# Hash attention with a squared-ReLU layer: the next chunk's x asked for one product later, and the last chunk's output stores on one queue

## The chip, the cores and the metric

The kernel runs on one core of one Trainium2 chip. The metric is the device time in microseconds (us) of one execution, here the median of three runs. The profiler's record of one further execution gives the span of that execution and the time of every instruction and transfer in it.

## What is computed

The first part is attention in which a query sees only the keys of its own hash bucket; its output, laid out as 3072 tokens by 512 features, is the input x of a two-layer network. All is in float32.

```
mask   = q_bucket[..., :, None] == k_bucket[..., None, :]
scores = where(mask, scale * q @ k.T, -1e9)          # 4 batches, 8 heads, 768 tokens, 64 features
attn   = softmax(scores) @ v
x      = attn.transpose(0, 2, 1, 3).reshape(3072, 512)
h      = x @ w_in                                    # 512 -> 2048
g      = max(h, 0) ** 2
out    = g @ w_out                                   # 2048 -> 512
```

## The kernel before

**Stages.** The first 330 us compute the attention, pair of heads by pair of heads, and write x to a buffer in device memory (x_all). Beside that the weights are brought in and written back in rearranged form (w_in_7, w_out_1). The rest of the time is the network. It runs over x in three chunks of 1024 tokens (`NCHUNK` = 3, index i). A chunk has a hidden stage, which makes g, and an output stage (`project`), which makes out.

**Fewer multiplications.** Both layers use a scheme of the Strassen and Winograd kind: a matrix product is split in 2 by 2 blocks and done with seven block products in place of eight, at the price of sums and differences of blocks on VectorE before and after. The output layer does this twice over. So an output stage is seven *output products*, k = 0 to 6, and each is itself seven groups of matmuls (function `product`, matmul at L712) that read seven weight tiles called leaf. In the order of TensorE's work the groups of one output product use the operands "11", "21", "t2", "t1", "t3", "22" and "t4". The last group, "t4", reads the block y21 of the product's operand after VectorE has subtracted t2 from it in place; this subtraction is the first line of `hook` (`minus(y21, y21, t2)`, executed at L516). Then `hook` makes the differences that the next product needs (`inner_sums`, L516), and the results of the groups are added up on VectorE (L1008), some copied out by ScalarE (L719).

**Order.** The instructions stand in the order in which the program writes them down (`tc.manual_schedule()`); each engine, and each engine's DMA queue, takes its own in that order. VectorE therefore does nothing that stands behind a waiting instruction, and the same holds for GpSimd (POOL), whose queue issues DMAs one after the other.

**What stands on POOL's queue in the first chunk's output stage.** For k = 0 to 3 `factor_units(k)` prepares a quarter of the inner weights of the later chunks: two loads of 256 KB into tiles named h (L837), then two stores of parts of them (L846), then `sums_a` on VectorE, which reads the loaded tiles (L510 to L513), then two stores of these sums (L846). On VectorE `sums_a` of product k stands ahead of that product's `hook`. In between stands `load_x(i + 1)` (L554), one DMA of 2 MB that brings the next chunk's x into the only x tile; before the change it is written down after product k = 0, so POOL's queue holds: the loads, stores and sums of k = 0, then x, then those of k = 1, of k = 2 and of k = 3. The next chunk's x is first read by `sum_x`, written down after product k = 3.

**Tiles h.** The tag h has five buffers (`NH`), which serve in turn the hidden stage, `factor_units` (four for each k) and the output tiles.

**Output.** When two halves of an output tile are done, `put_out` transposes it on VectorE (L1022) and stores it with four DMAs of 64 KB (L1029), most on SyncE's queue (SP), those of the lower right quarter, (ih, jh) = (1, 1), on POOL's; and in the last chunk the second and fourth DMA of the tile (1, 0) that is stored by `put_out` also on POOL's. The very last tile is stored by `put_last` in halves (L1049): two DMAs on SP's queue and two on ScalarE's (ACT). The leaf tiles are loaded by ACT's queue (L998), x's weights (w_unit) by SP's.

Of the kernel before, what the change touches and what calls it, by code (L numbers as in the profile page):

```python
# [34 lines left out]
def kernel(  # L35
# [10 lines left out]
    nc = tc.nc  # L46
# [20 lines left out]
    NCHUNK = B * S // NCH  # L67
# [447 lines left out]
    def minus(out, in0, in1):  # L515
        nc.vector.tensor_tensor(out=out, in0=in0, in1=in1, op=ALU.subtract)  # L516
# [34 lines left out]
    def load_x(i):  # L551

        x = p_c.tile([P, NFT, NCH], FP32, name="x")
        nc.gpsimd.dma_start(out=x, in_=x_all[:, :, i * NCH:(i + 1) * NCH])  # L554
        xs[i] = x, [p_c.tile([P, 2, NCH // 2], FP32, name=f"t_x{n}") for n in range(3)]
# [36 lines left out]
    with tc.manual_schedule():  # L592
# [21 lines left out]
        for pr in range(NP):  # L614
            a, b = 2 * pr, 2 * pr + 1
# [87 lines left out]
        def product(n, w, at, bt, c11, c12, c21, c22, hook=None):  # L703

            acc = [ps_m.tile([P, 512], FP32, name=f"acc{i}")[:, 0:w] for i in range(3)]

            def add(to, a, b, first, last):  # L710
                for i in range(n):
                    nc.tensor.matmul(  # L712
                        out=acc[to], lhsT=a(i), rhs=b(i), start=first and i == 0,
                        stop=last and i == n - 1, skip_group_check=True,
                    )

            def keep(of, name):
                t = p_r.tile([P, 512], FP32, name=name)[:, 0:w]
                nc.scalar.copy(out=t, in_=acc[of])  # L719
                return t  # L720

            add(0, at(0), bt["11"], True, False)
            one = keep(0, "one")
            add(1, at(1), bt["21"], True, True)
            if hook:
                hook()
            c11(acc[1], one)
            add(0, at(4), bt["t2"], False, False)
            two = keep(0, "two")
            add(2, at(3), bt["t1"], True, False)  # L730
            five = keep(2, "five")
            add(0, at(5), bt["t3"], False, False)
            three = keep(0, "three")
            add(2, at(6), bt["22"], False, True)
            c12(acc[2], two)
            c22(three, five)
            add(0, at(2), bt["t4"], False, True)
            c21(acc[0])
# [94 lines left out]
        def factor_units(n):  # L833

            src = [new_h().rearrange("p (a f c) -> p a f c", a=2, c=P) for _ in range(2)]
            for j in range(2):
                nc.gpsimd.dma_start(out=src[j], in_=w_in_7[j * NQ + n, :, 5:7])  # L837
            sums = [new_h().rearrange("p (a f c) -> p a f c", a=2, c=P) for _ in range(2)]
            sums_a(
                src[0][:, :, 0], src[0][:, :, 1], src[1][:, :, 0], src[1][:, :, 1],  # L840
                *(sums[j // 2][:, :, j % 2] for j in range(4)),
            )
            for lo, hi, t in (
                (0, 2, src[0]), (2, 3, src[1][:, :, 1:2]), (3, 5, sums[0]), (5, 7, sums[1])
            ):
                nc.gpsimd.dma_start(out=w_in_49[n, :, :, lo:hi], in_=t)  # L846

        def load_inner(i, n):

            if n < NQ:  # L850
                w_inner[i, n] = []
                for j, name in enumerate((("sum0", "sum3"), ("sum2", "sum1"))[n % 2]):
                    t = p_y.tile([P, 4, QN], FP32, name=name).rearrange("p a (b c) -> p (a b) c", c=P)
                    nc.sync.dma_start(out=t[:, 0:7], in_=w_in_49[n, :, j])
                    w_inner[i, n].append(t)
# [6 lines left out]
        def sums_inner(i):  # L862

            t_inner[i] = [p_y.tile([P, NQ, QN], FP32, name=f"t{m}", bufs=2) for m in range(2)]
            for j, t in enumerate(t_inner[i]):
                y11, y12, y21, y22 = quarters_x(i, j)
                minus(t[:, 0], y12, y11)
                minus(t[:, 1], y22, t[:, 0])
                minus(t[:, 2], y21, t[:, 1])
                minus(y12, y22, y12)  # L870
# [107 lines left out]
        def inner_sums(k, n=slice(0, NQ)):  # L978

            if k not in tens:  # L980
                tens[k] = [p_y.tile([P, NQ, QN], FP32, name=f"t{m}", bufs=2) for m in range(2)]
            t1, t2 = (t[:, n] for t in tens[k])
            b = OUTER[k][1]
            at = slice(NQ + n.start, NQ + n.stop)
            y11, y12, y21, y22 = b[:, n, 0:QN], b[:, n, QN:HN], b[:, at, 0:QN], b[:, at, QN:HN]
            minus(t1, y12, y11)
            minus(t2, y22, t1)
            minus(y12, y22, y12)
# [3 lines left out]
        def load_leaf(n, early=False):  # L992
            if n < 49:
                k, m = divmod(n, 7)
                m = LEAVES[m]
                leaves[k, m] = p_y.tile([P, NQ, P], FP32, name="leaf", bufs=NLEAF)
                queue = nc.sync if early else nc.scalar
                queue.dma_start(out=leaves[k, m], in_=w_out_49[OUTER[k][0], :, m])  # L998
# [19 lines left out]
        def put_out(i, ih, jh, n, o):  # L1018


            ot = p_r.tile([P, HN], FP32, name="h", bufs=NH)
            nc.vector.transpose(out=ot, in_=o)  # L1022
            m0 = ih * HD + n * P
            at = slice(i * NCH + jh * HN, i * NCH + (jh + 1) * HN)
            for a in range(P // 32):
                queue = nc.gpsimd if (ih, jh) == (1, 1) else nc.sync
                if (i, ih, jh) == (NCHUNK - 1, 1, 0) and a % 2:
                    queue = nc.gpsimd
                queue.dma_start(  # L1029
                    out=out[at, m0 + a * 32:m0 + (a + 1) * 32].rearrange("(c i) j -> i c j", i=32),  # L1030
                    in_=ot[a * 32:(a + 1) * 32].rearrange("i (c j) -> i c j", j=32),
                )
# [21 lines left out]
        def project(i):  # L1054
# [60 lines left out]
            for k in range(7):  # L1115
                b = OUTER[k][1]
                t1, t2 = tens.pop(k)
                if i == 0 and k < NQ:
                    factor_units(k)
                if k == 6 and more:  # L1120
                    load_inner(i + 1, 0)
                at = lambda m, k=k: lambda n: leaves[k, m][:, n]
                bt = {
                    "11": lambda n: b[:, n, 0:QN], "21": lambda n: b[:, NQ + n, 0:QN],
                    "22": lambda n: b[:, NQ + n, QN:HN], "t1": lambda n: t1[:, n],
                    "t2": lambda n: t2[:, n], "t3": lambda n: b[:, n, QN:HN],
                    "t4": lambda n: b[:, NQ + n, 0:QN],
                }

                def hook():  # L1130
                    y21 = b[:, NQ:NR, 0:QN]
                    minus(y21, y21, t2)
                    if k + 1 < 7 and k not in (1, 3):
                        inner_sums(k + 1)
                    if k == 6 and more:
                        sums_inner(i + 1)

                counted = []

                def a_with_load(m, k=k):  # L1140
                    load_leaf(7 * k + len(counted) + NLEAF - 2)
                    counted.append(m)
                    return at(m)

                use = uses[k]
                product(
                    NQ, QN, a_with_load, bt, lambda *p: use(0, *p), lambda *p: use(1, *p),
                    lambda p: use(2, p, None), lambda *p: use(3, *p), hook,
                )
                if k == 0 and i + 1 < NCHUNK:  # L1150
                    load_x(i + 1)
                if k in (3, 4) and i + 1 < NCHUNK:
                    sum_x(i + 1, 2 * k - 5)
                    sum_x(i + 1, 2 * k - 4)
                if k == 5 and i + 1 == NCHUNK:
                    guard()
                if k == 0:

                    for h in range(2):
                        at_h = slice(h * NQ, (h + 1) * NQ)  # L1160
                        minus(b11[:, at_h], b22[:, at_h], b_t[:, at_h])
                    inner_sums(2)
                if k == 2:

                    for h in range(2):
                        at_h = slice(h * NQ, (h + 1) * NQ)
                        minus(b_t[:, at_h], b21[:, at_h], b11[:, at_h])
                    inner_sums(4)
# [43 lines left out]
        for i in range(NCHUNK):  # L1212
# [32 lines left out]
            if i == NCHUNK - 1:  # L1245
                tops()
            project(i)
    fast.close()

# [234 lines left out]
```

## Time and profile before

| what | value |
|---|---|
| time, median of 3 runs | 881.38 us |
| lowest and highest of the 3 | 880.67 and 882.03 us |
| the profiled execution: time, span | 882.09 us, 880.3 us |
| x load (L554), three of them: issue to landing, shortest, median, longest | 9.1, 11.0, 12.6 us |
| loads of `factor_units` (L837), eight of them | 3.3, 5.6, 13.4 us |
| one `put_out` DMA (L1029): issue time on SP, shortest, median, longest | 315, 496, 877 ns |
| the same on POOL | 649, 649, 676 ns |
| last stores (L1049): issue to landing | 4.2 to 4.5 us |

In a line of the timeline the first number is the start in us from the span's start, the second the time until the end of the last of the merged instructions; then come engine, source line, operation, what is written from what is read, and the count. In brackets stands how long the engine had been idle before it and what ended that. A DMA's line on a queue is its issue alone; when it lands is told apart. The source lines are those of the kernel before.

### The profile page before, as it was taken

Reading aid. Unit: us, or ns where it says so; the run is one execution under the profiler, and the core shown is the slowest. Engines: PE = TensorE matmul, PEld = TensorE weight load, DVE = VectorE, ACT = ScalarE, POOL = GpSimd, SP = SyncE. Lnnn points to the kernel's source line nnn. Section 1 sums busy time; section 2 is a strip of 40 time slices with the busy share of each in tenths; the row PEclk is TensorE's granted clock in tenths of the full one; section 3 lists DMA queues with packets and bytes.
Section 4 is the critical chain, followed back from the end, with each engine's and each line's share of the span. In section 5 each row is a group of like instructions: output and inputs, shape, how many; then the busy total and the mean of one; then the engine's idle time right before and its main releaser. Section 6 shows DMA issues by size and latency. Waiting matters only on the chain.

```text
span 880.3 us, 12132 instructions
## 1 busy us (share of the span) xinstructions
PE 865.7 (98%) x4340; PEld 520.4 (59%) x4340; DVE 760.7 (86%) x1099; ACT 391.7 (44%) x673; POOL 106.9 (12%) x172
## 2 busy tenths in 40 slices
PE   8999999999999999999999999999999999999996
PEld 4444444444444444444678865556888755568885
DVE  5899999999999998888779968888889788888875
ACT  5988888888888851222211123332111233321110
POOL 2000000000000000554231021111000211110002
PEclk9999999999999999999999999999999999999999
DMA  9677977898878546999897665436846744355565
GB/s 187 122 151 134 231 151 152 180 259 220 179 169 217 162 130 207 297 262 289 289 342 255 175 160 173 164 114 229 288 145 187 171 159 156 128 167 152 159 172 107
DMA packets 224131, 167.09 MB, mean 190 GB/s; under 512 B 164448, under 2 KB 181344, under 8 KB 224064
## 3 DMA queue, kind: packets, MB, share of 16 engines
q1 hardware_dynamic: 189152, 87.19, 41.6%
q0 software_dynamic: 12528, 41.30, 15.0%
q10 hardware_dynamic: 22384, 37.76, 13.9%
q8 instruction: 36, 0.59, 0.3%
q14 instruction: 31, 0.25, 0.1%
HBM read 124.52 MB, written 41.68 MB: 189 GB/s over the span
## 4 chain that ended last, share of the span: by engine, by line
PE 95%; DVE 2%; ACT 1%; issue 1%; DVEq 0%
PE acc L712 40%; PE st L396 17%; PE acc L931 16%; PE xo L438 13%; PE acc L884 5%; PE hash L346 1%; PE tot L455 1%; DVE total L428 1%; ACT e L413 1%; ACT bits L356 1%; PE xo L326 0%; PE tp L309 0%; DVE s_in L516 0%; DVE out_piece L179 0%; DVE power L171 0%
## 5 line engine op out<-in xcount | busy, mean ns | idle before, releaser
L413 ACT ACTIVATE e<-st 128x1024 f32<-128x1024 f32 x192 | 145.1, 810 | 45.1 <-PE st L396 41.1
L396 PE MATMUL st<-feat,feat 64*128 64x512 f32 (+1 forms) x768 | 150.4, 484 | 0.0
L438 PE MATMUL xo<-e,v_nat 128*64 128x512 f32 (+1 forms) x768 | 134.8, 492 | 0.0
L712 PE MATMUL acc<-b,leaf 128*128 128x256 f32 x600 | 133.3, 380 | 1.5 <-issue 1.5
L712 PEld LDWEIGHTS acc<-b,leaf 128*128 128x128 f32 x600 | 113.9, 190 | 17.9 <-issue 2.7
L428 DVE TENSOR_TENSOR total<-total,e 128x1536 f32<-128x1536 f32 x64 | 112.4, 1757 | 5.2 <-ACT small L160 0.5
L438 PEld LDWEIGHTS xo<-e,v_nat 128*64 128x64 f32 x768 | 51.4, 136 | 82.4 <-issue 74.9
L931 PE MATMUL acc<-t_x,w_unit 128*128 128x512 f32 x192 | 90.2, 592 | 0.0
L396 PEld LDWEIGHTS st<-feat,feat 64*128 64x128 f32 x768 | 66.1, 189 | 33.3 <-issue 23.4
L712 PE MATMUL acc<-t,leaf 128*128 128x256 f32 x336 | 76.2, 380 | 0.0
L356 ACT ACTIVATE bits<-hash,lifts 32x384 bf16<-32x384 f32 x120 | 68.6, 572 | 3.2 <-issue 1.3
L712 PEld LDWEIGHTS acc<-t,leaf 128*128 128x128 f32 x336 | 63.8, 190 | 9.0 <-DVE t L516 0.5
L796 DVE SCALAR_TENSOR_TENSOR b<-h 128x512 f32<-128x512 f32 x96 | 65.7, 691 | 3.0
L396 PE MATMUL st<-bits,bits 64*128 64x256 bf16 (+1 forms) x384 | 63.1, 325 | 1.8 <-ACT e L413 1.4
L931 PE MATMUL acc<-x,w_unit 128*128 128x512 f32 x128 | 60.2, 592 | 0.0
L712 PE MATMUL acc<-x,w_unit 128*128 128x512 f32 x128 | 56.6, 594 | 0.0
L712 PE MATMUL acc<-b_t,leaf 128*128 128x256 f32 x240 | 53.8, 379 | 0.0
L931 PEld LDWEIGHTS acc<-t_x,w_unit 128*128 128x128 f32 x192 | 36.5, 190 | 28.8 <-issue 26.8
L719 ACT COPY two<-acc 128x256 f32<-128x256 f32 (+1 forms) x29 | 12.5, 431 | 87.8 <-PE acc L712 78.5
L719 ACT COPY one<-acc 128x256 f32<-128x256 f32 (+1 forms) x29 | 12.5, 431 | 86.6 <-PE acc L712 48.4
L712 PEld LDWEIGHTS acc<-b_t,leaf 128*128 128x128 f32 x240 | 45.6, 190 | 6.1
L396 PEld LDWEIGHTS <-bits 64*128 64x128 bf16 x384 | 23.4, 93 | 41.8 <-issue 37.9
(159 smaller groups left out, 1168.0 us busy)
## 6 DMA issues: line engine op xcount, KB each, us to landing
leaf<-w_out ACTq DMA_DIRECT2D x142, 256.0 KB, 3.1
w_unit<-w_in SPq DMA_DIRECT2D x16, 640.0 KB, 3.9
raw<-in_moe_w_in_dram SPq DMA_DIRECT2D x16, 512.0 KB, 5.6
raw<-in_moe_w_out_dram SPq DMA_DIRECT2D x16, 512.0 KB, 4.6
w_unit<-w_in SPq DMA_DIRECT2D x8, 896.0 KB, 8.0
w_out<-sums POOLq DMA_DIRECT2D x16, 448.0 KB, 6.8
sum<-w_in SPq DMA_DIRECT2D x16, 448.0 KB, 4.8
v_nat<-in_v_dram SPq DMA_DIRECT2D x16, 384.0 KB, 4.4
```

The source lines that it names most:

```text
L346: nc.tensor.matmul(out=banks[g * NR_B:(g + 1) * NR_B, h, 0:HS], lhsT=projs[rows], rhs=feat[pr, w][rows, c * HS:(c + 1) * HS], start=True, ...
L356: nc.scalar.activation(out=t[h * D:h * D + NR_B, c * HS:(c + 1) * HS], in_=hashed[pr, w][at, h, 0:HS], func=ACTF.Sign, scale=HUGE, bias=li ...
L396: nc.tensor.matmul(out=st[:, h, 0:hi - lo], lhsT=src[pr, 1][rows, key], rhs=src[pr, 0][rows, lo:hi], start=first, stop=not first,)
L413: nc.scalar.activation(out=e[:, :, lo:hi], in_=sts[i][:, :, 0:hi - lo], func=ACTF.Exp, scale=scale)
L428: nc.vector.tensor_tensor(out=totals[pr], in0=totals[pr], in1=weights[pr, kt][:, :, 0:S], op=ALU.add)
L438: nc.tensor.matmul(out=xo[h * D:(h + 1) * D, lo:hi], lhsT=nat[pr, "v_nat"][:, h, kt * D:(kt + 1) * D], rhs=weights[pr, kt][:, h, lo:hi], s ...
L455: nc.tensor.matmul(out=tot[g * 32:(g + 1) * 32, 0:HS], lhsT=ones, rhs=totals[pr][:, h, c * HS:(c + 1) * HS], start=True, stop=True,)
L712: nc.tensor.matmul(out=acc[to], lhsT=a(i), rhs=b(i), start=first and i == 0, stop=last and i == n - 1, skip_group_check=True,)
L719: nc.scalar.copy(out=t, in_=acc[of])
L796: nc.vector.scalar_tensor_tensor(out=out, in0=h, scalar=0.0, in1=h, op0=ALU.max, op1=ALU.mult)
L884: nc.tensor.matmul(out=out, lhsT=w[:, a], rhs=b, start=start, stop=stop, skip_group_check=True)
L931: nc.tensor.matmul(out=acc[to], lhsT=w[:, PLACE[a], f], rhs=bt[b](f), start=first and f == 0, stop=last and f == NFT // 2 - 1, skip_group_ ...
```

## The change

`load_x(1)`, the x of the second chunk, is written down after output product k = 1 of the first chunk, not after k = 0; for the other chunk it stays. In the last chunk all DMAs of `put_out` go on SP's queue: the eight of the quarter (1, 1) and two of the tile (1, 0) move there from POOL's. The first two chunks keep their queues.

```
             for a in range(P // 32):
-                queue = nc.gpsimd if (ih, jh) == (1, 1) else nc.sync
-                if (i, ih, jh) == (NCHUNK - 1, 1, 0) and a % 2:
-                    queue = nc.gpsimd
+
+                queue = nc.gpsimd if (ih, jh) == (1, 1) and i + 1 < NCHUNK else nc.sync
                 queue.dma_start(
...
-                if k == 0 and i + 1 < NCHUNK:
+                if k == (1 if i == 0 else 0) and i + 1 < NCHUNK:
                     load_x(i + 1)
```

## The prediction

> **What bounds the kernel now.** I read the engines' shares and the chain that ended last, then the first chunk's output stage on POOL, VectorE (DVE) and TensorE (PE), then the end.
>
> ```profile
> PE 865.7 (98%) x4340; PEld 520.4 (59%) x4340; DVE 760.7 (86%) x1099; ACT 391.7 (44%) x673; POOL 106.9 (12%) x172
> ...
> PE 95%; DVE 2%; ACT 1%; issue 1%; DVEq 0%
> ```
>
> TensorE sets the time nearly everywhere: what doesn't hold it up costs nothing, and each us in which it waits is a us of the kernel. So the question is whether it waits near the moved load. POOL's timeline there:
>
> ```profile
> 434.86 1.40 POOL L846 DMA_DIRECT2D w_in<-h  x2 [5.47 <-DVE h L512]
> 435.98 0.95 POOL L554 DMA_DIRECT2D x<-x_all  x1
> 436.75 1.28 POOL L837 DMA_DIRECT2D h<-w_in  x2
> 449.99 0.68 POOL L846 DMA_DIRECT2D w_in<-h  x1 [11.97 <-DMA h<-w_in]
> ```
>
> The loads of product 1 (L837) are issued right behind x's 2 MB, and their first store can't go until 449.99: the two small loads took over 13 us, where the median of the eight is 5.6. DVE and PE at that time:
>
> ```profile
> 447.42 1.22 DVE L516 TENSOR_TENSOR b_t<-b_t 128x1024 f32<-128x1024 f32 x1
> 450.75 0.42 DVE L510 TENSOR_TENSOR h<-h 128x256 f32<-128x256 f32 x1 [2.11 <-DMA h<-w_in]
> ...
> 452.22 1.22 DVE L516 TENSOR_TENSOR b<-b,t 128x1024 f32<-128x1024 f32 x1
> ...
> 459.11 0.42 DVE L510 TENSOR_TENSOR h<-h 128x256 f32<-128x256 f32 x1 [2.96 <-DMA h<-w_in]
> ...
> 460.58 1.22 DVE L516 TENSOR_TENSOR b_t<-b_t,t 128x1024 f32<-128x1024 f32 x1
> ```
> ```profile
> 448.31 3.75 PE L712 MATMUL acc<-b,leaf 128*128 128x256 f32 x16
> 453.54 1.97 PE L712 MATMUL acc<-b,leaf 128*128 128x256 f32 x8 [1.48 <-issue]
> 455.34 3.62 PE L712 MATMUL acc<-b_t,leaf 128*128 128x256 f32 x16
> ```
>
> DVE waits 2.11 us for product 1's loads, so the subtraction for group "t4" (L516 at 452.22) ends at 453.44, and PE starts that group at 453.54. The trace calls the gap "issue", but PE's start follows DVE's end by 0.1 us: this is the wait. DVE waits again, 2.96 us, for product 2's loads, and there PE loses nothing.
>
> [...] the loads behind x landed after it, while leaf loads of ACT's queue landed meanwhile. [...] In the window 436 to 451 us these were busy the whole time (share 1.00, 364 GB/s), so x, the two loads and the leaf loads divide one capacity.
>
> **The change part by part.** All on the profiled span, 880.3 us.
>
> *The unit.* Product 2 runs on PE from 455.34 to 467.43: 56 matmuls in 12.09 us, 216 ns each, 1.73 us a group; "t4", the seventh, is due 10.36 us after the start. Product 1 starts at 441.41 (16+16+24 matmuls after 429.32), so its "t4" is due at 451.77.
>
> *Removed: x ahead of product 1's loads.* They are then issued at 436.3 (end of the stores at 434.86) and, at 3.3 to 6.3 us, are in by 443. DVE needs them at 448.64 and goes on at once; the subtraction ends 2.11 us earlier, at 451.33, before 451.77. PE doesn't wait: product 2 starts at 451.77 + 1.73 = 453.50, not 455.34: **-1.84 us**.
>
> *Added: x ahead of product 2's loads.* Product 1's last two stores follow its sums, so they too go 2.11 us earlier: at 450.03, not 452.14. x's issue starts 1.12 us after the first such store (434.86 to 435.98), so at 451.15; product 2's loads follow 0.77 us later. Before, DVE went on 450.75 - 435.98 = 14.77 us after x's issue. The same queue content (two stores, x, two loads), and the same pace of leaf loads (PE reads a 256 KB leaf every 1.73 us), give the same delay: DVE goes on with product 2's sums at 451.15 + 14.77 = **465.92**, not at 459.11. It has nothing else to do: everything behind stands behind this wait, `hook` first of all.
>
> *First consequence.* The subtraction of product 2 ends 2.69 us after DVE goes on (459.11 to 461.80): at 468.61. PE's "t4" is due at 453.50 + 10.36 = 463.86 and starts at 468.71: **+4.85 us**. Product 3 starts at 470.44, against 467.43.
>
> *Second consequence.* Before, DVE worked from 459.11 to the end of product 3's subtraction at 477.27 (L516 at 476.05, 1.22 us) with 0.31 us of idle time, 17.85 us of work. PE's "t4" of product 3 was due at 467.43 + 10.36 = 477.79: 0.5 us of slack. Now the subtraction ends at 465.92 + 17.85 = 483.77, "t4" starts at 483.87, and was due at 470.44 + 10.36 = 480.80: **+3.07 us**.
>
> *After that.* Product 4's subtraction ended at 485.35 (L516 at 484.13), its "t4" was due 479.52 + 10.36 = 489.88: 4.5 us of slack. DVE is 6.5 us late, PE 6.1: it holds, and nothing is won back, since PE is at its pace from there on. Sum: -1.84 + 4.85 + 3.07 = **+6.08 us**.
>
> *Edits at nothing.* x itself: asked for 15.2 us later, it lands at about 464 and is first read at 481.73 (now later): 18 us of DVE's other work hide it. Product 3's loads come later as well, behind product 2's stores, by about 476; their sums, at 474.58 before, are now at 481. The eight stores of quarter (1, 1): their tiles are ready at 860.6 and 864.7; SP, at 496 ns each (877 at most), is done with them and its own eight by 870, and its next work is ready at 871.36. POOL's issues fall away and nobody waits for POOL.
>
> *The two stores of tile (1, 0).* On SP they stand ahead of the last two:
>
> ```profile
> 871.39 0.85 SPq L1029 DMA_DIRECT2D out_dram<-h  x2
> 873.05 0.83 SPq L1049 DMA_DIRECT2D out_dram<-h  x2
> ...
> 873.45 0.88 ACTq L1049 DMA_DIRECT2D out_dram<-h  x2
> ```
>
> (The third line is ACT's queue.) Two more at 0.5 us hold SP until 873.2 to 873.4, while its last tile is ready at 873.03: it issues 0.2 to 0.4 us later. ACT's last store, started at 873.86 and 4.2 us on its way, ends SP's closing wait at 878.1 anyhow, and SP's now land about level with it. I take **+0.2 us**; bounds -0.5 (POOL's last transfers no longer beside the others) and +1.0 (two issues in full).
>
> Sum: 6.08 + 0.2 = 6.3 us, span 886.6. The profiled execution was 882.09 us against a median of 881.38, so I add to the median: 881.38 + 6.3 = **887.7 us**.
>
> **The unknown cost** is when product 2's loads land. Below: x and the two loads are 2.5 MB, at 364 GB/s with no leaf load beside them 6.9 us, so not before 451.15 + 6.9 = 458.1. Above: 3 us over my value, if leaf loads take more of the capacity than before, 468.9. From 458 on each us costs one us: the sum is (time DVE goes on) - 459.8.
>
> **The rivals.**
> 1. *The collision doesn't bind: not slower.* If product 2's loads are in by 458.0, DVE is done in time for both "t4", and only the gain stays: 881.38 - 1.84 + 0.2 = 879.7. It decides at 459.8, 8.7 us after x's issue. For it: DVE waited 2.96 us here before without harm. Against it: that needs the leaf loads to yield nearly everything, while PE goes on reading leaves until 463.86.
> 2. *DVE catches up before product 3,* or the loads come earlier, near 462.8: -1.84 + 4.85 + 0.2, 884.6. Against it: 0.31 us of idle time in 18 us of DVE.
> 3. *More is lost:* the transfers take up to 3 us longer, or leaf tiles come late too: 890.0. Against it: in the collision before, PE lost under 0.2 us to anything but DVE.
>
> That the change doesn't do what it says is no case: the written order of the new kernel puts x on POOL between product 1's stores and product 2's loads.
>
> **How the numbers follow.** The forecast 0.62, rival 1 0.13, rival 2 0.13, rival 3 0.12. A measurement here tells 0.2% from no change, 1.8 us: slower is 0.62 + 0.13 + 0.12 = 0.87; rival 1 is 0.09 within it and 0.04 beyond. The range leaves out rival 1 (0.13) and half of rival 3 (0.06): from 883.0, rival 2 with the loads 1.6 us earlier, to 890.2.
>
> **What would show it.** Right: x on POOL at about 451.2; no wait of DVE at product 1, one of about 12 us at product 2, ended by h at about 466; PE gaps of about 4.8 and 3.1 us before the "t4" of products 2 and 3, none at product 1. Wrong: product 2's loads in before 460, or PE gaps that are waits for leaf. At the end SP's last pair starts at most 0.4 us later relative to its tile.

## The result, and the profile after

| kernel | median | lowest to highest | executions | span of the profiled one |
|---|---|---|---|---|
| before | 881.70 us | 880.67 to 882.10 us | 4 | 880.3 us |
| changed | 893.48 us | 893.03 to 894.29 us | 4 | 892.5 us |

The changed kernel is slower, by a ratio of 1.0135 (95% interval 1.012 to 1.015), which is 11.8 us. The prediction said 887.7 us, with a range from 883.0 to 890.2. The shares and the chain that ended last, from the page of the changed kernel:

```profile
PE 867.4 (97%) x4340; PEld 520.7 (58%) x4340; DVE 760.8 (85%) x1099; ACT 391.8 (44%) x673; POOL 100.8 (11%) x162
...
PE 93%; DVE 2%; issue 1%; ACT 1%; DMA 1%; ACTq 0%; DVEq 0%
```

TensorE is busy for 1.7 us more than before (865.7), on the same 4340 matmuls; for the other 10.5 of the 12.2 us by which the span grew it is idle. The chain gives up two points of PE. It ends with TensorE's last matmul, so it doesn't show what comes behind that; and the DMA in it is a load of k in the first 7 us of the kernel, which the change doesn't touch. Source lines from L1028 on are one lower than before (the change removes a line): `put_out` stores at L1028, `put_last` at L1048.

**The first chunk's output stage.** POOL's timeline of the changed kernel:

```profile
451.07 0.95 POOL L554 DMA_DIRECT2D x<-x_all  x1
451.83 1.29 POOL L837 DMA_DIRECT2D h<-w_in  x2
465.86 0.68 POOL L846 DMA_DIRECT2D w_in<-h  x1 [12.73 <-DMA h<-w_in]
```

x and the loads of product 2 go out one behind the other at 451, and the first store of these loads' tiles goes at 465.86. By the records x landed at 462.99 and the two loads behind it at 465.57 and 466.66, while six of ACT's leaf loads landed between 451.25 and 465.18. Before, with the DMA engines busy all the time from 436 to 451 us (share 1.00), x landed at 448.61, product 1's two loads at 449.71 and 450.73, and eight leaf loads between 436.68 and 449.96. VectorE in the same stage:

```profile
448.56 0.42 DVE L510 TENSOR_TENSOR h<-h 128x256 f32<-128x256 f32 x1
...
466.75 0.42 DVE L510 TENSOR_TENSOR h<-h 128x256 f32<-128x256 f32 x1 [12.64 <-DMA h<-w_in]
...
468.23 1.22 DVE L516 TENSOR_TENSOR b_t<-b_t,t 128x1024 f32<-128x1024 f32 x1
...
483.29 1.22 DVE L516 TENSOR_TENSOR b<-b,t 128x1024 f32<-128x1024 f32 x1
```

No wait stands at product 1 any more (448.56, no bracket), and one of 12.64 us at product 2. The two L516 lines are the subtractions for the groups "t4" of products 2 and 3. TensorE:

```profile
453.49 3.62 PE L712 MATMUL acc<-b_t,leaf 128*128 128x256 f32 x16
...
469.55 3.75 PE L712 MATMUL acc<-b_t,leaf 128*128 128x256 f32 x8 [5.53 <-issue]
473.09 3.70 PE L712 MATMUL acc<-b,leaf 128*128 128x256 f32 x16
...
484.61 5.42 PE L712 MATMUL acc<-b,leaf 128*128 128x256 f32 x24 [0.91 <-issue]
```

Product 2 starts 1.85 us earlier than before (453.49 for 455.34): that is the gain. Its "t4" starts at 469.55, when VectorE has subtracted, after 5.53 us of idle. The gap before the "t4" of product 3, at 484.61, is short, but product 3 itself starts 5.66 us late (473.09 for 467.43): besides the 5.53 us of idle, the eight matmuls of the group from 469.55 took 3.54 us and not 1.73. The windows view of that stretch (busy time and count of PE, of its weight loads, DVE, ACT and POOL, then the clock that TensorE was granted, as a share of its full rate, the DMA share and GB/s):

```profile
466.00:469.50 3.50, 0.00 (x0) 0.00 (x0) 2.71 (x6) 0.00 (x0) 2.60 (x5) 0.56 0.52 184
469.50:473.10 3.60, 3.56 (x9) 2.88 (x10) 3.57 (x4) 0.00 (x0) 1.17 (x3) 0.50 0.84 264
```

After the idle stretch the granted clock is 0.50 for 3.6 us; in the next 2.9 us it is 0.97. From product 4 on nothing is lost or won: TensorE is 6.89 us late there (its groups "t2" and "t1", in the kernel before and in the changed one):

```profile
482.97 3.62 PE L712 MATMUL acc<-t,leaf 128*128 128x256 f32 x16
```
```profile
489.86 3.62 PE L712 MATMUL acc<-t,leaf 128*128 128x256 f32 x16
```

**The end.** ScalarE copies out one half of TensorE's last results (VectorE the other), so this copy tells how late TensorE is when it is done. ACT's timeline of the kernel before, then of the changed kernel:

```profile
872.66 0.37 ACT L1044 COPY h<-acc 128x256 f32<-128x256 f32 x1 [4.29 <-PE acc L1039]
```
```profile
879.55 0.37 ACT L1043 COPY h<-acc 128x256 f32<-128x256 f32 x1 [4.29 <-PE acc L1038]
880.34 0.83 ACTq L1048 DMA_DIRECT2D out_dram<-h  x2
```

TensorE ends 6.89 us late, all of it from the first chunk. But from this copy to the end of the span passed 880.3 - 872.66 = 7.64 us before, and 892.5 - 879.55 = 12.95 us now: another 5.31 us, behind TensorE's last matmul. SP's timeline there, and then its waits from 855 us on (in total, times, longest):

```profile
883.57 2.57 SPq L1028 DMA_DIRECT2D out_dram<-h  x4
886.24 0.91 SPq L1048 DMA_DIRECT2D out_dram<-h  x2
```
```profile
SPq L1028 <- DMA out_dram<-h: 8.0, 1, 8.0
...
SPq L1282 <- SPq L1282: 2.4, 1, 2.4
```

The four stores at 883.57 are those of tile (1, 0). The tile was ready at 878.26:

```profile
877.55 0.71 DVE L1022 STREAM_TRANSPOSE h<-o 128x512 f32<-128x512 f32 x1
```

(VectorE's timeline; 877.55 + 0.71.) So SP neither waits for the tile nor is it busy issuing: for 8 us it waits for a store to land, and for 5.3 of them, from 878.26 to 883.52, a tile that is ready is held up. Which store that is, the instruction records of the trace tell; "waits" and "signals" are the numbers of the DMAs' semaphores, and a wait stands in the DMA itself or in an instruction ahead of it, which is listed only at 883.52:

```
start us   engine      instruction              waits    signals
870.24     SP          store, tile (0, 1)       109      109
870.92     SP          store, tile (0, 1)       100      100
871.62     SP          store, tile (0, 1)       105      105
872.17     SP          store, tile (0, 1)       106      106
872.77     SP          store, tile (1, 1)       107      107
873.27     SP          store, tile (1, 1)       108      108
873.82     SP          store, tile (1, 1)       109      109
875.05     SP          store, tile (1, 1)       100      100
880.34     ACT         store, last tile         102      102
880.72     ACT         store, last tile         104      104
883.52     SP          wait                     102
883.57     SP          store, tile (1, 0)                102
883.92     SP          store, tile (1, 0)       104      104
884.46     SP          store, tile (1, 0)       105      105
885.01     SP          store, tile (1, 0)       106      106
886.24     SP          store, last tile         107      107
886.72     SP          store, last tile         108      108
```

In this record the DMAs of SP and of ACT signal their landing with eight semaphores, 100, 102 and 104 to 109, dealt out in turn over both queues together (all 527 DMAs of SP and ACT fit such an order), and none of the 519 that take a number again starts before the DMA that had it last has landed; the shortest distance is 0.016 us. (GpSimd's 143 DMAs have other numbers, 111 to 118.) In SP's own sequence the number after 100 (at 870.92) is 105 (at 871.62). The 102 and 104 between them went to ACT's two stores of the *last* tile. So in the order of dealing these stand ahead of SP's last twelve stores, though in time they come after six of them; why they are dealt so early, no run tells. When the turn comes round to 102 again, it falls to SP's first store of tile (1, 0). Its tile is ready at 878.26, but it waits for a store that ACT can't issue until TensorE's last results are copied out, at 880.34, and that is 3.2 us on its way. The view of line L1048 in the changed kernel gives the landing times of the last tile's stores; the longest is the one waited for (880.34 to 883.50 by the records):

```profile
DMA to landing us min/median/max: 1.6/2.4/3.2
```

Before, SP's four last stores signal 109, 102, 105 and 106, and ACT's two 100 and 104: none waits for a later one.

Waits of SP for a landing on ACT's queue stood in the profile before as well, only not for the last tile. It is the first line of SP's waits over the whole kernel before:

```profile
SPq L1029 <- DMA leaf<-w_out: 190.2, 9, 73.3
```

What ended these nine waits was the landing of a leaf load of ACT's queue, which the stores don't read. Three of them, 176 us together, stand ahead of an output stage, when there is nothing to store yet; the other six, 1.2 to 3.3 us long, held up a store, and in all six the store and the leaf load have the same number. One of these in the records: SP's store at 853.41 signals 104, and it starts when ACT's leaf load with 104, issued at 849.15, has landed, at 853.39. So that queues wait for each other in this way could be read before the change was made.

### The profile page after: what moved, and what is told of

It reads as the page before. It is cut to its first block, busy times and chain, and to the rows that moved or that the text cites. A ratio compares the mean times of both kernels' runs of the same rounds, so it can differ in the third digit from the quotient of the medians.

```text
span 892.5 us, 12131 instructions
## 1 busy us (share of the span) xinstructions
PE 867.4 (97%) x4340; PEld 520.7 (58%) x4340; DVE 760.8 (85%) x1099; ACT 391.8 (44%) x673; POOL 100.8 (11%) x162
## 4 chain that ended last, share of the span: by engine, by line
PE 93%; DVE 2%; issue 1%; ACT 1%; DMA 1%; ACTq 0%; DVEq 0%
PE acc L712 39%; PE st L396 16%; PE acc L931 15%; PE xo L438 13%; PE acc L884 5%; PE hash L346 1%; PE tot L455 1%; DVE total L428 1%; DMA k_nat<-in_k_dram 1%; ACT e L413 1%; ACT bits L356 1%; DVE s_in L516 0%; DVE out_piece L179 0%; DVE power L171 0%; ACT small L160 0%
## 5 line engine op out<-in xcount | busy, mean ns | idle before, releaser
L712 PE MATMUL acc<-b_t,leaf 128*128 128x256 f32 x240 | 55.8, 388 | 5.5 <-issue 5.5
```

Source lines behind the costliest of these rows:

```text
L712: nc.tensor.matmul(out=acc[to], lhsT=a(i), rhs=b(i), start=first and i == 0, stop=last and i == n - 1, skip_group_check=True,)
```

## The experiments

All are compared with the kernel before on the same chip (881.84, 881.60 and 881.71 us in the three groups). "Last copy" is ScalarE's copy of TensorE's last result, "behind it" the span less this time; the copies vary by some 0.5 us for a reason that lies ahead of the changed stage (product 1 of the first chunk starts between 441.22 and 441.76 us in the twelve profiles).

| kernel | median us | ratio, 95% interval | last copy us | behind it us |
|---|---|---|---|---|
| before (profile above) | 881.70 | | 872.66 | 7.64 |
| changed | 893.48 | 1.0135, 1.012 to 1.015 | 879.55 | 12.95 |
| x_only | 887.62 | 1.0067, 1.005 to 1.0084 | 879.59 | 7.71 |
| stores_only | 887.78 | 1.0072, 1.0055 to 1.0089 | 872.64 | 13.16 |
| stores_11 | 886.62 | 1.0056, 1.004 to 1.0073 | 873.18 | 12.72 |
| stores_10 | 881.62 | 1.0000, 0.9991 to 1.0009 | 873.18 | 7.42 |
| loads_first | 881.07 | 0.9991, 0.9983 to 1.0 | 871.58 | 7.72 |
| x_k2 | 882.59 | 1.001, 1.0002 to 1.0018 | 875.43 | 7.47 |
| stores_last_pool | 881.82 | 1.0001, 0.9993 to 1.001 | 872.31 | 7.59 |
| loads_first0 | 880.98 | 0.9991, 0.9983 to 1.0 | 871.33 | 7.67 |
| after_last_pool | 887.45 | 1.0069, 1.0052 to 1.0086 | 877.93 | 7.67 |
| both_cured | 880.98 | 0.9993, 0.9984 to 1.0002 | 871.55 | 7.65 |

The two columns at the right separate the causes: x moves only the first of them, the stores only the second.

### One half of the change alone: x_only and stores_only

x_only makes only the second edit of the change, stores_only only the first.

```
x_only:
-                if k == 0 and i + 1 < NCHUNK:
+                if k == (1 if i == 0 else 0) and i + 1 < NCHUNK:
stores_only:
-                queue = nc.gpsimd if (ih, jh) == (1, 1) else nc.sync
-                if (i, ih, jh) == (NCHUNK - 1, 1, 0) and a % 2:
-                    queue = nc.gpsimd
+                queue = nc.gpsimd if (ih, jh) == (1, 1) and i + 1 < NCHUNK else nc.sync
```

> The second chunk's x asked for one product later; all stores as before. Theory: this is the whole of the loss in the first chunk, 6.9 us (VectorE goes on at about 466.7 in place of 459.1), and nothing at the end: 881.7 + 6.9 = 888.6 us. Rival (the stage at the end suffers from a TensorE that had to wait, or the two parts add up in another way): anything over 891.

> The ten stores of the last chunk on SyncE's queue; x asked for as before. Theory: SyncE's first store of the last tile but one waits for a completion semaphore that ScalarE's first store of the very last tile has taken, so it starts about 5 us after its tile is ready and the end comes 5.3 us later: 887.0 us. Rival (the tail of the changed kernel is a consequence of the first chunk's delay): 882.

x_only lost 5.8 us, less than the 6.9 expected, stores_only 5.9; together 11.7, against 11.8 for both at once, so they add up. In x_only VectorE's timeline has the wait of the changed kernel:

```profile
466.78 0.42 DVE L510 TENSOR_TENSOR h<-h 128x256 f32<-128x256 f32 x1 [12.32 <-DMA h<-w_in]
```

In stores_only SP has the wait at the end, though TensorE is on time (SP's waits, then its timeline):

```profile
SPq L1028 <- DMA out_dram<-h: 7.1, 1, 7.1
```
```profile
879.41 0.93 SPq L1048 DMA_DIRECT2D out_dram<-h  x2
```

ACT's last stores go out at 873.43 there, as before (873.45); SP's last pair at 879.41, where before it went at 873.05. So the loss at the end doesn't need the late TensorE.

### Which stores do it: stores_11 and stores_10

stores_11 moves only the eight stores of quarter (1, 1), stores_10 only the two of tile (1, 0).

```
stores_11:
-                queue = nc.gpsimd if (ih, jh) == (1, 1) else nc.sync
+                queue = nc.gpsimd if (ih, jh) == (1, 1) and i + 1 < NCHUNK else nc.sync
stores_10:
-                if (i, ih, jh) == (NCHUNK - 1, 1, 0) and a % 2:
-                    queue = nc.gpsimd
```

> Of the ten stores only the eight of the quarter (1, 1) go to SyncE's queue, the two of the tile (1, 0) stay on GpSimd's; x as before. The eight are done 4 us before the next work of SyncE is ready. In this program's order of semaphores ScalarE's last stores again take the two that SyncE's stores of tile (1, 0) need. Theory (semaphore taken over): SyncE waits about 5 us there, then has two stores fewer to issue than with all ten: 885 to 886 us. Rival (issue time of SyncE, or the short pieces of the stores right before the end): the eight cost nothing, 881.7.

> Only the two stores of tile (1, 0) go to SyncE's queue, right ahead of the last stores; the eight of quarter (1, 1) stay on GpSimd's; x as before. In this program's order ScalarE's last stores take semaphores that no later store of SyncE needs. Theory (semaphore taken over): no wait but the issue of two stores, 881.9 to 882.4 us. Rival (issue time of SyncE, or short pieces right before the end): most of the 5.3 us is here, 885 to 887.

stores_10 costs nothing that can be measured, and SP has no wait for a landing at out. Its SP timeline shows what the prediction had priced, four issues and then the last pair, which goes 0.78 us after the last copy (873.18) and before went 0.39 after it:

```profile
871.92 1.95 SPq L1027 DMA_DIRECT2D out_dram<-h  x4
873.96 0.93 SPq L1047 DMA_DIRECT2D out_dram<-h  x2
```

By the records ACT's last stores signal 100 and 104 there, and SP's six last ones 109, 102 and 105 to 108: none waits for a later one.

stores_11 loses 4.8 of the 5.9 us of stores_only (886.62 us, where 885 to 886 was expected), ACT's last stores and SP's two of tile (1, 0) both signal 102 and 104, and SP has the wait:

```profile
SPq L1029 <- DMA out_dram<-h: 9.1, 2, 8.7
```

So it is the eight stores of quarter (1, 1), the ones priced at nothing, that shift the dealing. They don't hold SP by their own issue: in the changed kernel SP was done with the last of them at 875.54 (issued at 875.05, 0.49 us), 2.7 us before tile (1, 0) was ready.

### Another queue for ACT's half of the last tile: stores_last_pool and after_last_pool

If the wait is a matter of the shared semaphores, it must go when ACT's two stores take others. Both kernels put them on GpSimd's queue, in `put_last`; stores_last_pool is stores_only with this edit, after_last_pool the changed kernel with it.

```
-                (nc.sync if col else nc.scalar).dma_start(
+                (nc.sync if col else nc.gpsimd).dma_start(
```

> All ten stores on SyncE's queue as in the change, but the half of the very last tile that ScalarE's queue stored goes out on GpSimd's queue, whose DMAs signal other semaphores; x as before. SyncE's queue holds exactly what it holds with the ten stores alone. Theory (semaphore taken over): SyncE's first store of tile (1, 0) starts when its tile is ready, the end is 0 to 1 us later than before: 881.8 to 882.8 us. Rival (what stands on SyncE's queue is too much): 887 to 888 as with the ten stores alone.

> The changed kernel, but the two stores of the very last tile that ACT issued go on GpSimd's queue. Theory (two independent losses: the collision of x with product 2's loads, some 5.9 us, and SP's wait on ACT's last store, some 5.9 us): only the first stays, 881.5 + 5.9 = 887.4 us, no wait of SP for a landing at out_dram before its stores of tile (1, 0). Rival (the end's loss comes from ten more stores on one queue, or from TensorE being late): it stays near 893.5 us.

stores_last_pool is at the time of before, with all ten stores on SP's queue. SP's timeline:

```profile
846.65 26.34 SPq L1028 DMA_DIRECT2D out_dram<-h  x28
873.09 0.93 SPq L1048 DMA_DIRECT2D out_dram<-h  x2
```

after_last_pool keeps the loss of x_only and loses that of stores_only; behind the last copy it takes 7.67 us, as before. In the records of both, SP's last stores take all eight numbers in turn, none missing, and none waits for the other half of the last tile, though the same data go out. The rival, ten more stores on one queue, would have stayed at the changed kernel's time. That the edit cures because of the semaphores and not for another property of GpSimd's queue rests on the records shown above: no run kept ACT's queue and changed only the numbers.

### Loads ahead of x: loads_first and loads_first0

If the collision is a matter of POOL's order, product 2's loads must be in early once they stand ahead of x, at the same place. `factor_units` is split: `factor_loads(n)` takes its two tiles and loads them, and `factor_units` uses what is loaded. loads_first has x after product 1, as the change has it; loads_first0 leaves x after product 0 and puts product 1's loads ahead.

```
+        def factor_loads(n):
+            early[n] = [new_h().rearrange("p (a f c) -> p a f c", a=2, c=P) for _ in range(2)]
...
loads_first:
-                if k == 0 and i + 1 < NCHUNK:
+                if k == (1 if i == 0 else 0) and i + 1 < NCHUNK:
+                    if i == 0:
+                        factor_loads(2)
                     load_x(i + 1)
loads_first0:
                 if k == 0 and i + 1 < NCHUNK:
+                    if i == 0:
+                        factor_loads(1)
                     load_x(i + 1)
```

> x asked for after product 1 as in the change, but the two loads of product 2 are written down ahead of it, so on GpSimd's queue they are no longer behind the 2 MB; stores as before. Theory (order within the queue): VectorE waits at no product up to 2, or goes on there by 458, TensorE loses nothing in the stage: 881.8 - 1.8 = 880.0 us. Rival (the DMA engines are full, whoever stands first): VectorE still goes on only after 460 and the time stays above 883.

> x asked for after product 0 as in the kernel before, but with the two loads of product 1 written down ahead of it; stores as before. Theory: the 2.1 us wait of VectorE at product 1 and the 1.8 us of TensorE behind it are gone, and product 2's loads come after x is in: 880.0 us, a kernel faster than both. Rival (the loads only change places with x and something later waits): 881.8.

In loads_first the wait at product 2 is 3.90 us, which TensorE doesn't see (VectorE's timeline):

```profile
458.23 0.42 DVE L510 TENSOR_TENSOR h<-h 128x256 f32<-128x256 f32 x1 [3.90 <-DMA h<-w_in]
```

TensorE is 1.63 us ahead when product 2 starts (453.71) and 1.08 us at the last copy; the rest is given back in products 2 and 3 of the same stage (product 4 starts at 478.44, 1.07 us ahead), where weight loads of TensorE wait 0.6 us for leaf tiles. The expectation had nothing lost there. In loads_first0 the last copy is 1.33 us earlier. The times gain less, about 0.6 us (881.07 and 880.98 against 881.60, where 880.0 was expected): the profiled execution before was itself 0.5 us over that median. The intervals touch 1; this is at most 0.2% faster, and the fastest found.

### One product later still: x_k2

x after product 2, so that it collides with product 3's loads.

```
-                if k == 0 and i + 1 < NCHUNK:
+                if k == (2 if i == 0 else 0) and i + 1 < NCHUNK:
```

> x asked for one product later still, after product 2: now the loads of product 3 stand behind it; stores as before. Theory: no wait at products 1 and 2; x's issue at about 459.9, VectorE needs product 3's loads at about 472.7 and gets them 14.8 to 15.6 us after x's issue, at 474.7 to 475.5; the last group of product 3, due at 475.95, starts at 477.5 to 478.3: a loss of 1.5 to 2.3 us against the gain of 1.84: 881.4 to 882.3 us. Rival (each product later costs as much as the first): 888 or more.

The expectation, 881.4 to 882.3 us, was a little too good. VectorE and TensorE in x_k2:

```profile
476.05 0.43 DVE L510 TENSOR_TENSOR h<-h 128x256 f32<-128x256 f32 x1 [2.83 <-DMA h<-w_in]
```
```profile
478.84 7.07 PE L712 MATMUL acc<-b,leaf 128*128 128x256 f32 x24 [2.39 <-DVE b L516]
```

The delay from x's issue to VectorE's going on is again near 15 us (POOL issued x at 460.59, so 15.46; in the changed kernel 451.07 to 466.75, 15.68), and VectorE waits only 2.83 us, since it had other work by then. But the 2.39 us of idle on TensorE is followed by another stretch at half clock (the windows view):

```profile
478.80:480.60 1.80, 1.76 (x4) 1.51 (x5) 1.70 (x5) 0.00 (x0) 0.04 (x1) 0.50 1.00 388
480.60:482.40 1.80, 1.80 (x6) 1.43 (x5) 1.70 (x5) 0.00 (x0) 0.00 (x0) 0.56 0.18 68
```

In sum TensorE loses 4.5 us there in this execution, of which 1.7 are the slow matmuls (24 in 6.90 us for 5.18), and after the gain of 1.7 ends 2.8 us late. The profiled execution was the slowest of 13 (884.68 us); the median is 1.0 us above before.

### Both causes taken away: both_cured

The changed kernel with the edits of loads_first and after_last_pool.

> The changed kernel with both causes taken away: product 2's loads ahead of x (x stays after product 1), and the last tile's two ACT stores on GpSimd's queue. Theory: nothing of the loss stays, 881.0 to 881.7 us, DVE waiting about 4 us at product 2 and no wait of SP at the end. Rival (a further cause in the change that neither cure touches): over 883 us.

It is at 880.98 us, and both of its columns at the right agree with those of loads_first. VectorE's wait at product 2, and SP's last stores:

```profile
458.18 0.42 DVE L510 TENSOR_TENSOR h<-h 128x256 f32<-128x256 f32 x1 [4.19 <-DMA h<-w_in]
```
```profile
870.28 1.95 SPq L1036 DMA_DIRECT2D out_dram<-h  x4
872.32 0.93 SPq L1056 DMA_DIRECT2D out_dram<-h  x2
```

x where the change puts it, all stores on SP's queue, and nothing of the 11.8 us is left: no third cause shows.

## Why the prediction was right in one half and wrong in the other

**"Removed: x ahead of product 1's loads", -1.84.** Right: -1.85, with no wait at product 1.

**"Added: x ahead of product 2's loads".** The mechanism was right. x was issued at 451.07 (predicted 451.15); VectorE went on at 466.75, 0.83 us later than the 465.92 said. The delay behind x's issue was 15.68 us and not the 14.77 taken over from before. It varies between executions: with x at the same place it was 15.36 us in x_only and 14.15 in after_last_pool. The value was in the bounds of 458.1 to 468.9. (The lower bound is 0.3 us too low: x and the two loads are 2560 KB of 1024 bytes, which take 7.2 us at 364 GB/s, not 6.9. Nor is 364 GB/s, the mean of the window from 436 to 451 us before, the most that was moved: in the changed kernel it was 401 from 458 to 464. So the bound is an estimate.)

**"First consequence", +4.85.** The group was due at 453.49 + 10.36 = 463.85 and started at 469.55: 5.70. The 0.85 too few are the 0.83 of the step before.

**"Second consequence", +3.07.** The sum was right, its nature not. The gap of 3.07 us did not appear; there is one of 1.15 (484.61, due 473.09 + 10.36 = 483.45). The other 1.9 us are matmuls at half clock after the idle. They cost nothing in addition, because "t4" of product 3 waits for VectorE in any case, and VectorE's 17.85 us of work from 466.75 on set its start: predicted 17.95 us after VectorE goes on (465.92 to 483.87), measured 17.86. The same 17.86 us stand in x_only (466.78 to 484.64 by the records), where the slow matmuls took up nearly the whole gap. The prediction had not asked for the clock, which was granted at 0.50 from 466.42 to 473.25 us here. In x_k2, in one execution, it was 0.50 after a single gap of 2.39 us, and there the slow matmuls were not hidden; in the gap of 1.48 us before the change and behind it (452.06 to 457.10) it was 1.00.

**"After that", nothing.** Right: 6.89 us late at product 4 and still at the last copy. Sum of the first chunk: predicted 6.08, measured 6.89 in the profile, 5.8 in the medians of x_only (whose profiled execution, also 6.93 late at the last copy, was 1.4 us over its median). By the prediction's own formula, 466.75 - 459.8 = 6.95. That 6.08 lies so near is in part luck: the delay of 14.77 us, taken from one execution, happens to lie inside the spread of 14.15 to 15.68 us.

**"Edits at nothing", the eight stores, and "The two stores of tile (1, 0)", +0.2 with bounds -0.5 and +1.0.** This is the step that failed: measured +5.31 in the profile, and +5.9 in the medians of stores_only. What was priced was SP's issue time, and for the two stores that was right: in stores_10 SP's last pair is 0.39 us later against the last copy, where 0.2 to 0.4 was said, and the time is that of before. What was not asked is whether the moved DMAs change what *other* DMAs wait for. The bound above counted two issues in full; a wait of SP for a landing was not among the cases, so the range ended below the time.

That a change of queue changes nothing but issue time was the author's estimate; no run had shown it. In the list above each DMA that takes a number again starts after the landing of the one before (SP's store with 102 at 883.57, after 883.50), and which DMA the number was shared with was what cost the 5.3 us. Here the choice of queue also decided whose landing a DMA waited for: 5.9 us in stores_only, with a wait of 7.1 us for a landing. Neither the issue time of ten more stores on SP's queue nor their bandwidth accounts for it, since stores_last_pool has the same ten there and sends out the same data in 881.82 us.

**The rivals.** Neither of the first two happened. "More is lost" went in the right direction, at 890.0, but longer transfers account for 0.8 us of the profile at most, and the rest came from a wait that it doesn't name.

## What to carry to other kernels

Before a DMA is moved between queues that share completion semaphores, look in the queue's waits for landings that its DMAs have no use for (nine here before the change), and write down which semaphore each DMA near it takes and which earlier DMA it waits for. Where the dealing order differed from the order of time, here at the last stores, a store that was ready waited 5.3 us for a later one, and nothing hid it. Before a large load is moved, look at what stands behind it on its queue, and put the small loads that an engine needs soon ahead of it (VectorE's wait at product 2: 12.64 us in the changed kernel, 3.90 in loads_first). In a gap on TensorE, look at the granted clock and count the slow matmuls behind it (1.8 us behind 5.53 in the changed kernel, 1.7 behind 2.39 in x_k2) as well as the gap, unless something else sets the next start.

## What the runs showed that was not expected

- **Half clock after short idle.** After 5.53 us of idle the granted clock was 0.50 for 3.6 us, with eight matmuls in 3.54 us for 1.73; after 2.39 us of idle in x_k2 it was 0.50 and then 0.56 over 3.6 us. It fell while TensorE was still idle: the windows view has 0.50 from 466.42 to 473.25 us in the changed kernel and from 478.77 to 482.19 us in x_k2. The gap of 0.91 us before 484.61 was not followed by a slow stretch (1.00 from 484.61 to 488.20).
- **SP's closing wait.** SP waits 2.4 to 3.5 us after its last stores in every run; it is 3.5 us before and 2.4 in the changed kernel. Because of that the end lost 5.3 us and not the 6.3 by which SP's last pair is late against TensorE. The prediction took ACT's last landing to end this wait. That can't hold in the changed kernel, where the wait ends at 890.27 and the last landing was at 888.35. The wait stands right behind a branch (L1282), and the record of DMA packets has one transfer of kind "instruction" in it, 8 KB at 888.72; that SP waited for it isn't shown. What ends the wait stays open.
- **Two issues on SP took over twice the usual 0.5 us.** In the changed kernel one store at 873.82 took 1.18 us to issue and that at 885.01 took 1.13, where the median is 0.5. The second lies on the path.
